# Random-feature attention, a dense four-expert layer and a cosine layer on one core: float64 weight halves spaced by TensorE columns instead of by quanta

## The chip, the cores and the metric

The kernel runs on one core of one Trainium2 chip. The metric is the device time of one execution in microseconds (us). Five engines work side by side, each through its own list of instructions in order: TensorE (PE in the profile, PEld its weight loads), VectorE (DVE), ScalarE (ACT), GpSimd (POOL) and SyncE (SP). GpSimd's and SyncE's queues also issue DMA transfers between the chip's memory and the on-chip buffer. An instruction that has to wait holds up all that stand behind it in its engine's list.

## The reference, cut to what matters

```
q_p, k_p = phi(q), phi(k)                     # phi(x) = exp(h - max h) / sqrt(m), h = x omega^T - |x|^2 / 2
attn = (q_p (k_p^T v)) / (q_p sum(k_p) + 1e-6)       # 2 x 8 heads x 576 tokens x 64
x = attn.reshape(1152, 512)
p = domain_probs / (sum(domain_probs) + 1e-9)
out = 0
for e in range(4):
    out += p[:, e] * (relu(x @ w1[e]) @ w2[e])       # 512 -> 1024 -> 512
h = out @ w_in                                       # 512 -> 2048, w_in is float64
result = (h * cos(h)) @ w_out                        # 2048 -> 512, w_out is float64
```

All inputs are float32, but `w_in` and `w_out` are float64. Each factor of a product is split into a high and a low part, and three products (high by high, high by low, low by high) stand for one.

## The kernel before

After the attention part, TensorE goes through six **rounds** of the same shape: rounds 0 to 3 are the four experts, rounds 4 and 5 the two halves of the cosine layer's 2048 hidden columns (`E = 4`). From round 1 on a round has two parts. **Part one** (`first_product`) makes the hidden values, 1152 tokens in three chunks of 384; seven products and two plain ones per pair of hidden blocks take the place of a plain block product, so VectorE adds their results into `h` (L449), some from banks that TensorE opens again later (`g_..c`). **Part two** (`Second`) multiplies by the second weight: for each of nine token tiles of 128, ScalarE makes the high part `sth` (L523) of a half of the hidden values and VectorE the low part `stl` (L524), up to two or three halves ahead; TensorE's third matmul of a half reads `stl`. VectorE adds the result into `acc` (L584).

The program is written by generators. Each `yield` on TensorE's stream is a **quantum** of six matmuls: 6 x 384 = 2304 columns in part one, 6 x 512 = 3072 columns in part two. Part one has 44 quanta, part two 36, a round 80 (round 0 has 84). `plan()` names for each background job the quantum at which it starts; from then on it advances one `yield` per quantum. So the order of each engine's list is fixed by these numbers, and the engines run through it as their waits allow. Below, "quantum 41" of a round counts from its first; 0 to 43 are part one.

The background jobs are these. `load_v2` and `load_a` bring the next experts' weights through SP and split them (ScalarE L106, VectorE L108); `load_a` also makes the sums of weight blocks that the seven products need (four additions on L140, a split on L106 and L108). `convert64` turns the float64 weights into float32: 32 **halves** of 128 x 512 numbers, 512 KB each. Halves of kind `a` are of `w_in`, those of kind `v` of `w_out`. A half goes like this:

- quantum q: GpSimd's queue issues the load of `f64r` (L176 or L182)
- q + 5 (`LEAD`): ScalarE copies the absolute value of the high words out of `f64r` into `f64t` (L186). In this text that is *the copy* of a half
- one quantum later VectorE's L190 and L193, two later L198 and L201, three later L204, the last reader of `f64r`; for kind `a` also L209, and one quantum later the store `ka` (L211)
- kind `v` only: five quanta behind the copy ScalarE makes the high part from `f64a` into `f64t` (L215); six behind, VectorE makes the low part in `f64b` (L217, L218), and the two stores `kv_..h` and `kv_..l` are issued (L220)

There is one buffer each of `f64r`, `f64t`, `f64a` and `f64b` (pool `c1`, `bufs=1`; two halves of round 0 use a second pool). A load therefore waits for L204 of the half before it, and a copy waits for the store that still reads `f64t`. The eight halves of round 0 have written-out quanta. The other 24 start at quantum 80 of round 0, spaced 8 quanta apart for kind `a` (`A_GAP`) and 10 for kind `v` (`V_GAP`); eight `v` halves fall into round 1, eight `a` halves into round 2, eight `v` halves into the end of round 2 and round 3.

Of the kernel before, what the change touches and what calls it, by code (L numbers as in the profile page):

```python
# [26 lines left out]
def performer_moe_kernel(ctx, tc, q, k, v, omega, probs, w1, w2, w_in, w_out, out):  # L27
    nc = tc.nc
# [14 lines left out]
    CW = TC * P  # L43
# [16 lines left out]
    late = {}  # L60
# [31 lines left out]
        return units[key]  # L92

    LEAD = 5
    A_GAP, V_GAP = 8, 10

    def wait(n):
        for _ in range(n):
            yield
# [55 lines left out]

    kept = {}

    def convert64(pool, key, z):

        kind, e, u = key
        n = UW // 2
        hf = e - E
        if key not in kept:
            nm = "_".join(map(str, key))
            kept[key] = (
                dram.tile([P, UW], F32, tag=f"k{nm}", name=f"k{nm}")
                if kind == "a"
                else tuple(dram.tile([P, UW], F32, tag=f"k{nm}{s}", name=f"k{nm}{s}") for s in "hl")  # L170
            )
        raw = pool.tile([P, n, 2], U32, tag="f64r", name="f64r")
        lw, hw = raw[:, :, 0], raw[:, :, 1]
        if kind == "a":
            c0 = hf * F + (z * NPF + u) * P
            nc.gpsimd.dma_start(  # L176
                out=raw.rearrange("p (k f) t -> p k f t", f=P),
                in_=w_in32[:, c0 : c0 + P, :].rearrange("(k p) f t -> p k f t", p=P),
            )
        else:  # L180
            r0 = hf * F + u * 256 + z * P
            nc.gpsimd.dma_start(out=raw, in_=w_out32[r0 : r0 + P, :, :])  # L182
        yield from wait(LEAD)

        t = pool.tile([P, n], U32, tag="f64t", name="f64t")
        nc.scalar.activation(t.bitcast(F32), hw.bitcast(F32), ACTF.Abs)  # L186
        yield
        a = pool.tile([P, n], U32, tag="f64a", name="f64a")
        b = pool.tile([P, n], F32, tag="f64b", name="f64b")
        nc.vector.tensor_scalar(  # L190
            out=t.bitcast(F32), in0=t.bitcast(F32), scalar1=2.0**-15, scalar2=None, op0=ALU.max
        )
        nc.vector.tensor_scalar(  # L193
            out=a, in0=t, scalar1=0x07FFFFFF, scalar2=3,
            op0=ALU.bitwise_and, op1=ALU.logical_shift_left,
        )
        yield
        nc.vector.scalar_tensor_tensor(  # L198
            out=a, in0=hw, scalar=0xC0000000, in1=a, op0=ALU.bitwise_and, op1=ALU.bitwise_or
        )  # L200
        nc.vector.tensor_scalar(out=t, in0=a, scalar1=0xFF800000, scalar2=None, op0=ALU.bitwise_and)  # L201
        yield
        af = a.bitcast(F32)
        nc.vector.scalar_tensor_tensor(  # L204
            out=b, in0=lw, scalar=2.0**-52, in1=t.bitcast(F32), op0=ALU.mult, op1=ALU.mult
        )
        half = slice(z * n, (z + 1) * n)
        if kind == "a":
            nc.vector.tensor_tensor(out=af, in0=af, in1=b, op=ALU.add)  # L209
            yield  # L210
            nc.gpsimd.dma_start(out=kept[key][:, half], in_=af)  # L211
            return
        yield from wait(2)
        hi = t.bitcast(F32)
        nc.scalar.activation(t.bitcast(F32R), af, ACTF.Copy)  # L215
        yield
        nc.vector.tensor_tensor(out=af, in0=af, in1=hi, op=ALU.subtract)  # L217
        nc.vector.tensor_tensor(out=b.bitcast(F32R), in0=af, in1=b, op=ALU.add)  # L218
        for part, dst in zip((hi, b), kept[key]):
            nc.gpsimd.dma_start(out=dst[:, half], in_=part)  # L220

    def load_v64(e, u):

# [412 lines left out]
    QE = [84] + (E + 1) * [80]  # L636
    starts = [{} for _ in range(E + 2)]

    def start_at(e, q, make, *args):
        while q >= QE[e]:  # L640
            q -= QE[e]
            e += 1
        starts[e].setdefault(q, []).append(lambda: make(*args))

    def plan():
        start_at(0, 45, token_sums)
        start_at(0, 60, token_sum3)
        for e in range(1, E + 2):
            for p, q in enumerate((60, 70) if e == 1 else (50, 60)):
                start_at(e - 1, q, load_a, e, p)  # L650
            start_at(e, 0, load_v2 if e < E else load_v64, e, 0)
            start_at(e, 6, load_a, e, 2)
            start_at(e, 9, load_v2 if e < E else load_v64, e, 1)
            start_at(e, 17, load_a, e, 3)
            start_at(e, 23, load_v2 if e < E else load_v64, e, 2)
            start_at(e, 26, load_v2 if e < E else load_v64, e, 3)

        halves = [
            (kind, e, u, z)
            for e in (E, E + 1) for kind in "av" for u in range(NU) for z in range(2)  # L660
        ]
        when = [(q, "c1") for q in (21, 31, 41, 51, 61, 71)] + [(q, "c2") for q in (23, 33)]
        n = len(halves) - len(when)
        gaps = [A_GAP if h[0] == "a" else V_GAP for h in halves[len(when) :]]
        when += [(80 + sum(gaps[:i]), "c1") for i in range(n)]
        for (kind, e, u, z), (q, ring_) in zip(halves, sorted(when)):
            start_at(0, q, lambda k=(kind, e, u), z=z, r=ring_: convert64(late[r], k, z))
        start_at(E - 1, 58, second_x, 1)
        start_at(E - 1, 69, second_sums)
        start_at(E, 3, second_x, 0)  # L670

    plan()

    def dense():
# [39 lines left out]
    with tc.tile_pool(name="at1", bufs=1) as at1, tc.tile_pool(name="at2", bufs=2) as at2:  # L714
# [280 lines left out]
        for b in range(B):  # L995
            nc.sync.dma_start(
                out=pr[:, b * R : (b + 1) * R, :],
                in_=probs[b * S : b * S + SB, :].rearrange("(p r) e -> p r e", r=R),
            )
            nc.sync.dma_start(  # L1000
                out=pr[b * L : (b + 1) * L, NTILE - 1, :], in_=probs[b * S + SB : (b + 1) * S, :]
# [48 lines left out]
        for s in range(NPR + 3):  # L1050
# [39 lines left out]
            if 2 <= s <= NPR + 1:  # L1090
                b, hp = pairs[s - 2]
# [29 lines left out]
            if s == 1:  # L1121
# [4 lines left out]
                    out=pn, in0=pr, in1=psum_.to_broadcast([P, NTILE, E]), op=ALU.mult  # L1126
# [38 lines left out]
```

## Time and profile before

| what | value |
|---|---|
| median of 3 runs | 679.45 us (678.39 to 679.77) |
| the profiled execution's own time | 678.58 us |
| its span, first to last instruction | 676.8 us |
| TensorE busy | 664.8 us (98%) |
| VectorE busy | 513.5 us (76%) |
| ScalarE busy | 314.1 us (46%) |
| GpSimd busy | 169.5 us (25%) |
| granted TensorE clock, mean | 0.999 |

The page gives busy times; matmuls overlap in the pipeline, so that 98% busy does not mean that no time is lost: a short stop between two matmuls is covered by the recorded length of the first. The view of windows cuts the span at given times; the windows below are cut at the first matmul of a part, so that the length of a window is what the part took. The view of waits names, for an engine that stood idle, the instruction or the transfer that released it. The timeline shows single instructions with their start, their length and, in brackets, the idle time ahead of them.

### The profile page before, as it was taken

To read this page: it belongs to the slowest core of one execution; us is meant where nothing else is said; L and a number is where in the kernel's file an instruction comes from. 1 tells how busy PE (TensorE), PEld (TensorE's weight loads), DVE (VectorE), ACT (ScalarE), POOL (GpSimd) and SP (SyncE) were. 2 spreads that over 40 slices of the span, in tenths; PEclk is the share of its full clock that TensorE was granted. 3 is DMA by queue.
4 is the path that set the end of the run, shared out by engine and by line. 5 is a ranking of instruction groups with operands and counts; after the bars stand their busy time and mean duration, and the time that the engine had idled before them with its cause. 6 is when DMAs were issued, how large, how long until landed. Compare 5 with 4: busy or idle time off the path is not lost.

```text
span 676.8 us, 10000 instructions
## 1 busy us (share of the span) xinstructions
PE 664.8 (98%) x3665; PEld 608.3 (90%) x3665; DVE 513.5 (76%) x945; ACT 314.1 (46%) x626; POOL 169.5 (25%) x220
## 2 busy tenths in 40 slices
PE   8999999999999899999899999999999999999998
PEld 7999998998899888899787899888999888999887
DVE  6998645788867779679677789788778785396962
ACT  4777763244243344335324245454355664355540
POOL 8778420110111111111110111100034340143420
PEclk9999999999999999999999999999999999999999
DMA  8654001233444624427433536320711000700111
GB/s 196 182 140 124 33 1 63 94 105 114 118 131 125 214 67 138 142 57 209 124 94 79 166 119 196 110 78 17 279 59 36 1 0 4 308 1 1 47 47 47
DMA packets 51217, 68.86 MB, mean 102 GB/s; under 512 B 15072, under 2 KB 35808, under 8 KB 51168
## 3 DMA queue, kind: packets, MB, share of 16 engines
q1 hardware_dynamic: 42576, 38.82, 18.4%
q0 software_dynamic: 8448, 29.37, 14.1%
q8 instruction: 29, 0.48, 0.3%
q14 instruction: 20, 0.16, 0.1%
q10 hardware_dynamic: 144, 0.03, 0.0%
HBM read 53.27 MB, written 14.94 MB: 101 GB/s over the span
## 4 chain that ended last, share of the span: by engine, by line
PE 78%; DVE 10%; DMA 6%; issue 3%; ACT 2%; POOL 0%; POOLq 0%; ACTq 0%; DVEq 0%
PE g L551 37%; PE g L402 15%; DMA f64r<-in_moe_w_in_dram 3%; PE num L936 2%; PE kv L907 2%; DVE h L449 2%; PE pj_q L830 1%; PE g_0a L402 1%; PE g_0c L402 1%; DVE f64a L198 1%; PE g_1c L402 1%; PE g_1a L402 1%; PE pj_k L830 1%; DVE f64b L204 1%; PE g_3c L402 1%
## 5 line engine op out<-in xcount | busy, mean ns | idle before, releaser
L523 ACT ACTIVATE sth<-h 128x512 fp32r<-128x512 f32 x72 | 44.6, 629 | 51.9 <-PE g L551 48.8
L524 DVE SCALAR_TENSOR_TENSOR stl<-h,sth 128x512 fp32r<-128x512 f32 x72 | 48.8, 685 | 17.3 <-ACT sth L523 17.1
L186 ACT ACTIVATE f64t<-f64r 128x512 f32<-128x512 f32 x32 | 21.3, 666 | 66.3 <-DMA f64r<-in_moe_w_in_dram 33.6
L551 PE MATMUL g<-v_0h,stl 128*128 128x512 f32 (+1 forms) x110 | 43.2, 393 | 4.7 <-DVE stl L524 4.7
L108 DVE TENSOR_TENSOR stl<-h,sth 128x512 fp32r<-128x512 f32 x36 | 35.3, 983 | 13.8 <-ACT sth L106 13.8
L551 PE MATMUL g<-v_3h,sth 128*128 128x512 f32 (+1 forms) x110 | 42.7, 388 | 0.0
L551 PE MATMUL g<-v_0h,sth 128*128 128x512 f32 (+1 forms) x110 | 42.6, 387 | 0.0
L551 PE MATMUL g<-v_2h,stl 128*128 128x512 f32 (+1 forms) x110 | 42.6, 387 | 0.0
L551 PE MATMUL g<-v_2h,sth 128*128 128x512 f32 (+1 forms) x110 | 42.5, 386 | 0.0
L551 PE MATMUL g<-v_0l,sth 128*128 128x512 f32 (+1 forms) x110 | 42.5, 386 | 0.0
L551 PE MATMUL g<-v_1h,stl 128*128 128x512 f32 (+1 forms) x110 | 42.4, 386 | 0.0
L551 PE MATMUL g<-v_1h,sth 128*128 128x512 f32 (+1 forms) x110 | 42.4, 386 | 0.0
L551 PE MATMUL g<-v_3h,stl 128*128 128x512 f32 (+1 forms) x110 | 42.4, 386 | 0.0
L551 PE MATMUL g<-v_1l,sth 128*128 128x512 f32 (+1 forms) x110 | 42.4, 386 | 0.0
L551 PE MATMUL g<-v_2l,sth 128*128 128x512 f32 (+1 forms) x110 | 42.4, 385 | 0.0
L551 PE MATMUL g<-v_3l,sth 128*128 128x512 f32 (+1 forms) x110 | 42.4, 385 | 0.0
L343 ACT ACTIVATE h<-g 128x384 f32<-128x384 f32 x48 | 23.2, 487 | 39.2 <-PE g L402 39.0
L182 POOL DMA_DIRECT2D f64r<-in_moe_w_out_dram x16 | 8.6, 539 | 120.5 <-DVE f64b L204 67.1
L353 POOL TENSOR_TENSOR cosa<-cosa,cosr 128x384 f32<-128x384 f32 x16 | 18.7, 1171 | 78.3 <-DVE cosr L350 78.3
L176 POOL DMA_DIRECT2D f64r<-in_moe_w_in_dram x16 | 12.3, 770 | 78.6 <-DVE f64b L204 59.7
L551 PEld LDWEIGHTS g<-v_0h,stl 128*128 128x128 f32 x110 | 20.6, 188 | 11.3 <-DVE stl L524 7.3
L106 ACT ACTIVATE sth<-h 128x512 fp32r<-128x512 f32 x36 | 22.4, 623 | 16.1 <-PE g L551 12.5
(407 smaller groups left out, 2134.3 us busy)
## 6 DMA issues: line engine op xcount, KB each, us to landing
ra<-in_moe_w_dram SPq DMA_DIRECT2D x32, 256.0 KB, 3.3
rv<-in_moe_w_dram SPq DMA_DIRECT2D x16, 512.0 KB, 3.8
f64r<-in_moe_w_in_dram POOLq DMA_DIRECT2D x16, 512.0 KB, 4.5
f64r<-in_moe_w_out_dram POOLq DMA_DIRECT2D x16, 512.0 KB, 4.4
ka<-f64a POOLq DMA_DIRECT2D x16, 256.0 KB, 4.1
ra<-ka SPq DMA_DIRECT2D x8, 512.0 KB, 4.2
kt<-in_k_dram SPq DMA_DIRECT2D x8, 256.0 KB, 2.9
qt<-in_q_dram SPq DMA_DIRECT2D x8, 256.0 KB, 3.3
```

What stands on the lines that cost most here:

```text
L106: nc.scalar.activation(hi, src, ACTF.Copy)
L108: eng.tensor_tensor(out=lo, in0=src, in1=hi.bitcast(F32), op=ALU.subtract)
L186: nc.scalar.activation(t.bitcast(F32), hw.bitcast(F32), ACTF.Abs)
L343: nc.scalar.activation(dst, src, ACTF.Copy)
L353: nc.gpsimd.tensor_tensor(out=vv, in0=vv, in1=kk, op=ALU.subtract)
L402: nc.tensor.matmul(dst, x[:, o], y[:, kk, :], start=start and n == 0, stop=stop and n == 3 * kn - 1, skip_group_check=reopen,)
L449: nc.vector.tensor_tensor(out=dst, in0=x, in1=y, op=ALU.add)
L523: nc.scalar.activation(hi, src, ACTF.Relu)
L524: nc.vector.scalar_tensor_tensor(out=lo, in0=src, scalar=0.0, in1=hi.bitcast(F32), op0=ALU.max, op1=ALU.subtract)
L551: nc.tensor.matmul(g, x[:, p, :], y[:, o : o + w], start=n == 0, stop=n == 3 * FT - 1)
L830: nc.tensor.matmul(pj[:, i * 256 : (i + 1) * 256], a[:, cs], b_, start=z == 0, stop=z == 2)
L907: nc.tensor.matmul(kvp[:, h, :], phk[:, h * R + r, :], ve[:, h * R + r, :], start=r == 0, stop=r == R - 1)
```

## The change

A half is no longer spaced by quanta but by columns of TensorE's work. `columns_to(q)` counts the columns that TensorE has before quantum q, `quantum_at(columns)` finds the first quantum at or behind a number of columns, both counted from quantum 80 of round 0. The starts of the 24 later halves are 22000 columns apart for kind `a` and 26000 for kind `v`, and their copy stands 14000 columns behind their load, instead of five quanta. The halves of round 0 ahead of quantum 80 stay as they are. In rounds 1 to 3 the loads thus move by -1 to +5 quanta, and the time from load to copy is 5 to 7 quanta. The store of the high part is issued in the program right behind L215 and not behind L218; in the new file the lines below the removed one have numbers lower by one (L217 and L218 keep theirs).

```diff
--- before.py
+++ after.py
@@ -92,7 +92,6 @@
         return units[key]
 
     LEAD = 5
-    A_GAP, V_GAP = 8, 10
 
     def wait(n):
         for _ in range(n):
@@ -155,7 +154,7 @@
 
     kept = {}
 
-    def convert64(pool, key, z):
+    def convert64(pool, key, z, lead):
 
 
 
@@ -180,7 +179,7 @@
         else:
             r0 = hf * F + u * 256 + z * P
             nc.gpsimd.dma_start(out=raw, in_=w_out32[r0 : r0 + P, :, :])
-        yield from wait(LEAD)
+        yield from wait(lead)
 
         t = pool.tile([P, n], U32, tag="f64t", name="f64t")
         nc.scalar.activation(t.bitcast(F32), hw.bitcast(F32), ACTF.Abs)
@@ -213,11 +212,11 @@
         yield from wait(2)
         hi = t.bitcast(F32)
         nc.scalar.activation(t.bitcast(F32R), af, ACTF.Copy)
+        nc.gpsimd.dma_start(out=kept[key][0][:, half], in_=hi)
         yield
         nc.vector.tensor_tensor(out=af, in0=af, in1=hi, op=ALU.subtract)
         nc.vector.tensor_tensor(out=b.bitcast(F32R), in0=af, in1=b, op=ALU.add)
-        for part, dst in zip((hi, b), kept[key]):
-            nc.gpsimd.dma_start(out=dst[:, half], in_=part)
+        nc.gpsimd.dma_start(out=kept[key][1][:, half], in_=b)
 
     def load_v64(e, u):
 
@@ -636,6 +635,15 @@
     QE = [84] + (E + 1) * [80]
     starts = [{} for _ in range(E + 2)]
 
+    A_GAP, V_GAP, LOAD64 = 22000, 26000, 14000
+
+    def columns_to(q):
+        full, q = divmod(q - 84, 80)
+        return (full * 80 + q + max(0, q - 44) / 3 + full * 12) * 6 * CW
+
+    def quantum_at(columns):
+        return next(q for q in range(80, sum(QE)) if columns_to(q) - columns_to(80) >= columns)
+
     def start_at(e, q, make, *args):
         while q >= QE[e]:
             q -= QE[e]
@@ -662,9 +670,10 @@
         when = [(q, "c1") for q in (21, 31, 41, 51, 61, 71)] + [(q, "c2") for q in (23, 33)]
         n = len(halves) - len(when)
         gaps = [A_GAP if h[0] == "a" else V_GAP for h in halves[len(when) :]]
-        when += [(80 + sum(gaps[:i]), "c1") for i in range(n)]
+        when += [(quantum_at(sum(gaps[:i])), "c1") for i in range(n)]
         for (kind, e, u, z), (q, ring_) in zip(halves, sorted(when)):
-            start_at(0, q, lambda k=(kind, e, u), z=z, r=ring_: convert64(late[r], k, z))
+            lead = LEAD if q < 80 else quantum_at(columns_to(q) - columns_to(80) + LOAD64) - q
+            start_at(0, q, lambda k=(kind, e, u), z=z, r=ring_, l=lead: convert64(late[r], k, z, l))
         start_at(E - 1, 58, second_x, 1)
         start_at(E - 1, 69, second_sums)
         start_at(E, 3, second_x, 0)
```

How the lists move, at three places. First ScalarE's list at the end of part one and the start of part two of round 2: `h10`, `h00` and `h01` are hidden values, `sth` the high parts for part two, and the rows that write `f64t` are the copies of two halves of `w_in`. Before:

```order
L453 ACTIVATE h10_3278<-g1_2_3a_3638 128x384
L186 ACTIVATE f64t_3646<-f64r_3602 128x512
L343 ACTIVATE h00_3276<-g1_2_0_0_3_3691 128x384
L523 ACTIVATE sth_3705<-h00_3276 128x512
L343 ACTIVATE h01_3277<-g1_2_0_1_3_3709 128x384
L523 ACTIVATE sth_3723<-h01_3277 128x512
L186 ACTIVATE f64t_3727<-f64r_3680 128x512
L365 ACTIVATE h10_3278<-g1_2_3a_3638 128x384
L523 ACTIVATE sth_3756<-h00_3276 128x512
L523 ACTIVATE sth_3778<-h01_3277 128x512
L523 ACTIVATE sth_3796<-h00_3276 128x512
```

Now:

```order
L452 ACTIVATE h10_3278<-g1_2_3a_3637 128x384
L342 ACTIVATE h00_3276<-g1_2_0_0_3_3678 128x384
L522 ACTIVATE sth_3692<-h00_3276 128x512
L185 ACTIVATE f64t_3696<-f64r_3635 128x512
L342 ACTIVATE h01_3277<-g1_2_0_1_3_3698 128x384
L522 ACTIVATE sth_3716<-h01_3277 128x512
L364 ACTIVATE h10_3278<-g1_2_3a_3637 128x384
L522 ACTIVATE sth_3748<-h00_3276 128x512
L522 ACTIVATE sth_3764<-h01_3277 128x512
L185 ACTIVATE f64t_3775<-f64r_3722 128x512
L522 ACTIVATE sth_3784<-h00_3276 128x512
```

The first of the two copies stood ahead of the first `sth` and stands behind it; the second one has moved from between the second and third `sth` to ahead of the fifth.

Second, VectorE's list in part two of round 2, from the sum into `acc2` on: `rs3_0` are the sums of weight blocks for round 3, `stl` the low parts that TensorE waits for, and `f64t`, `f64a` and `f64b` belong to a half. Before:

```order
L584 SCALAR_TENSOR_TENSOR acc2_85<-g2_2_2_0_3834,pn_86,acc2_85 128x512
L140 TENSOR_TENSOR rs3_0_3876<-ra3_0_3822 128x256
L140 TENSOR_TENSOR rs3_0_3876<-rs3_0_3876,ra3_0_3822 128x256
L524 SCALAR_TENSOR_TENSOR stl_3887<-h10_3278,sth_3886 128x512
L140 TENSOR_TENSOR rs3_0_3876<-ra3_0_3822 128x256
L140 TENSOR_TENSOR rs3_0_3876<-ra3_0_3822,rs3_0_3876 128x256
L108 TENSOR_TENSOR a_3_0l_3874<-ra3_0_3822,a_3_0h_3873 128x1024
L524 SCALAR_TENSOR_TENSOR stl_3908<-h11_3279,sth_3907 128x512
L190 TENSOR_SCALAR f64t_3899<-f64t_3899 128x512
L193 TENSOR_SCALAR f64a_3914<-f64t_3899 128x512
L584 SCALAR_TENSOR_TENSOR acc3_1730<-g2_2_3_0_3879,pn_86,acc3_1730 128x512
L108 TENSOR_TENSOR s_3_0l_3912<-rs3_0_3876,s_3_0h_3911 128x1024
```

Now:

```order
L583 SCALAR_TENSOR_TENSOR acc2_85<-g2_2_2_0_3826,pn_86,acc2_85 128x512
L189 TENSOR_SCALAR f64t_3853<-f64t_3853 128x512
L192 TENSOR_SCALAR f64a_3862<-f64t_3853 128x512
L139 TENSOR_TENSOR rs3_0_3869<-ra3_0_3815 128x256
L139 TENSOR_TENSOR rs3_0_3869<-rs3_0_3869,ra3_0_3815 128x256
L523 SCALAR_TENSOR_TENSOR stl_3880<-h10_3278,sth_3879 128x512
L197 SCALAR_TENSOR_TENSOR f64a_3862<-f64r_3801,f64a_3862 128x512
L200 TENSOR_SCALAR f64t_3853<-f64a_3862 128x512
L139 TENSOR_TENSOR rs3_0_3869<-ra3_0_3815 128x256
L139 TENSOR_TENSOR rs3_0_3869<-ra3_0_3815,rs3_0_3869 128x256
L203 SCALAR_TENSOR_TENSOR f64b_3863<-f64r_3801,f64t_3853 128x512
L208 TENSOR_TENSOR f64a_3862<-f64a_3862,f64b_3863 128x512
```

The five instructions of a half up to the one that writes `f64b` stand between the four additions into `rs3_0`; before, they came behind them.

Third, GpSimd's queue at the start of round 1: `f64r` are loads of halves, `kv_..h` and `kv_..l` the stores of the high and the low part. Before:

```order
L182 DMA f64r_2492<-in_moe2_w_out_dram 128x1024
L220 DMA kv_4_0h_2390<-f64t_2437 128x512
L220 DMA kv_4_0l_2391<-f64b_2448 128x512
L182 DMA f64r_2604<-in_moe2_w_out_dram 128x1024
L220 DMA kv_4_0h_2390<-f64t_2542 128x512
L220 DMA kv_4_0l_2391<-f64b_2555 128x512
L182 DMA f64r_2715<-in_moe2_w_out_dram 128x1024
L220 DMA kv_4_1h_2602<-f64t_2648 128x512
```

Now:

```order
L215 DMA kv_4_0h_2390<-f64t_2437 128x512
L181 DMA f64r_2493<-in_moe2_w_out_dram 128x1024
L219 DMA kv_4_0l_2391<-f64b_2448 128x512
L215 DMA kv_4_0h_2390<-f64t_2561 128x512
L181 DMA f64r_2622<-in_moe2_w_out_dram 128x1024
L219 DMA kv_4_0l_2391<-f64b_2575 128x512
L181 DMA f64r_2739<-in_moe2_w_out_dram 128x1024
L215 DMA kv_4_1h_2620<-f64t_2694 128x512
```

The first two stores of a high part stand ahead of a load that they stood behind; the third still stands behind it.

## Rows read from the trace of the kernel before

**Rows 1.** Windows: stretch, length; busy time (count) of PE, PEld, DVE, ACT, POOL; clock, DMA.

```profile
186.56:233.92 47.36, 46.39 (x266) 45.75 (x265) 36.62 (x63) 20.40 (x33) 6.16 (x12) 1.00 0.48 144
233.92:284.42 50.50, 49.56 (x217) 40.39 (x217) 40.14 (x69) 19.47 (x30) 7.21 (x13) 1.00 0.43 135
284.42:330.24 45.82, 45.82 (x265) 45.81 (x264) 37.52 (x66) 19.14 (x30) 5.28 (x9) 1.00 0.45 127
330.24:384.17 53.93, 50.16 (x218) 40.24 (x217) 39.75 (x70) 17.00 (x27) 6.45 (x11) 1.00 0.38 108
384.17:429.95 45.78, 45.78 (x265) 45.78 (x264) 39.70 (x67) 21.52 (x34) 7.55 (x14) 1.00 0.48 151
528.98:578.10 49.12, 49.12 (x217) 40.47 (x217) 33.58 (x51) 26.50 (x50) 12.64 (x10) 1.00 0.06 22
```

**Rows 2.** TensorE's waits, whole span: microseconds in total, times, longest.

```profile
PE g L551 <- DVE stl L524: 4.7, 6, 1.4
...
PE g_2c L402 <- DVE h L449: 0.6, 1, 0.6
```

**Rows 3.** ScalarE's waits from 284 to 384 us (round 2).

```profile
ACT f64t L186 <- DMA f64r<-in_moe_w_in_dram: 26.3, 7, 6.8
```

**Rows 4.** ScalarE's waits from 186.56 to 284 us (round 1).

```profile
ACT f64t L186 <- DMA kv_0h<-f64t: 4.3, 2, 4.2
```

**Rows 5.** Timeline of ScalarE, copies of halves: start, length, what, [idle before, releaser].

```profile
325.38 0.67 ACT L186 ACTIVATE f64t<-f64r 128x512 f32<-128x512 f32 x1 [4.88 <-DMA f64r<-in_moe_w_in_dram]
...
334.70 0.66 ACT L186 ACTIVATE f64t<-f64r 128x512 f32<-128x512 f32 x1 [5.21 <-DMA f64r<-in_moe_w_in_dram]
...
344.10 0.66 ACT L186 ACTIVATE f64t<-f64r 128x512 f32<-128x512 f32 x1 [6.80 <-DMA f64r<-in_moe_w_in_dram]
...
354.84 0.66 ACT L186 ACTIVATE f64t<-f64r 128x512 f32<-128x512 f32 x1 [5.21 <-DMA f64r<-in_moe_w_in_dram]
...
366.73 0.66 ACT L186 ACTIVATE f64t<-f64r 128x512 f32<-128x512 f32 x1 [5.29 <-DMA f64r<-in_moe_w_out_dram]
...
423.91 0.66 ACT L186 ACTIVATE f64t<-f64r 128x512 f32<-128x512 f32 x1 [3.57 <-DVE h L449]
```

**Rows 6.** Timeline of GpSimd: loads of halves and a store.

```profile
206.75 0.54 POOL L182 DMA_DIRECT2D f64r<-in_moe_w_out_dram  x1 [8.25 <-DVE h L449]
...
207.28 0.54 POOL L220 DMA_DIRECT2D kv_0h<-f64t  x1
...
362.17 0.54 POOL L182 DMA_DIRECT2D f64r<-in_moe_w_out_dram  x1 [10.57 <-DVE f64b L204]
```

**Rows 7.** Timeline of VectorE, second part of round 2.

```profile
353.36 0.42 DVE L140 TENSOR_TENSOR rs<-ra,rs 128x256 f32<-128x256 f32 x1
...
356.66 0.42 DVE L190 TENSOR_SCALAR f64t<-f64t 128x512 f32<-128x512 f32 x1
...
357.46 0.75 DVE L584 SCALAR_TENSOR_TENSOR acc<-g,pn,acc 128x512 f32<-128x512 f32 x1
...
358.12 1.22 DVE L108 TENSOR_TENSOR s_0l<-rs,s_0h 128x1024 fp32r<-128x1024 f32 x1
...
359.25 0.69 DVE L198 SCALAR_TENSOR_TENSOR f64a<-f64r,f64a 128x512 uint32<-128x512 uint32 x1
...
360.32 0.68 DVE L524 SCALAR_TENSOR_TENSOR stl<-h,sth 128x512 fp32r<-128x512 f32 x1
...
360.92 0.68 DVE L204 SCALAR_TENSOR_TENSOR f64b<-f64r,f64t 128x512 f32<-128x512 uint32 x1
```

**Rows 8.** Timeline of TensorE around its longest stop in part two of round 2.

```profile
336.76 0.39 PE L551 MATMUL g<-v_0l,sth 128*128 128x512 f32 x1
...
338.46 0.50 PE L551 MATMUL g<-v_0h,stl 128*128 128x512 f32 x1 [1.31 <-DVE stl L524]
```

**Rows 9.** DMA issues: engine, operation, count, KB each, median us to landing.

```profile
f64r<-in_moe_w_in_dram POOLq DMA_DIRECT2D x16, 512.0 KB, 4.5
...
kv_0h<-f64t POOLq DMA_DIRECT2D x4, 256.0 KB, 5.2
```

## The prediction

> **What bounds the kernel now.** I read the windows first, then who made TensorE wait, then whom that engine waited for.
>
> Cut at the first matmul of a part, the windows show that TensorE runs its parts at a fixed pace except in three of them. Part one takes 45.82 us in round 2 and 45.78 in round 3, so its floor is 45.80, or 1.041 us a quantum; part two takes 49.12 us in round 4, where no half is converted, or 1.364 us a quantum [rows 1]. Over these floors stand part one of round 1 by 47.36 - 45.80 = 1.56 us, part two of round 1 by 50.50 - 49.12 = 1.38, and part two of round 2 by 53.93 - 49.12 = 4.81. Together 7.75 us. This is all that a better order of background work can give back in these rounds; the granted clock is 1.00 in every one of them.
>
> The reader is to see next that it is `stl`, VectorE's low part, that TensorE waits for (4.7 us that the view shows, six times), and in part one a sum on L449 [rows 2]. The view shows less than the windows, since a recorded matmul (0.39 us, [rows 8]) is longer than TensorE's pace of 49.12 / 216 = 0.23 us a matmul and covers the start of a stop. VectorE in turn is late because ScalarE is: in round 2 ScalarE stood idle for 26.3 us, seven times, at the copy of a half, for the load of `f64r` [rows 3]. All `sth` of part two stand in the same list behind that copy.
>
> Why are the loads late? Follow one half around. Its copy starts at 354.84 [rows 5]; VectorE's L204 ends at 360.92 + 0.68 = 361.60 [rows 7]; GpSimd, which waited for just that, issues the next load at 362.17 [rows 6]; the next copy starts at 366.73 [rows 5]. From the end of L204 to the next copy it is 5.13 us, of which the transfer takes 4.5 [rows 9]. The whole cycle took 9.32 us (325.38 to 334.70), then 9.40, 10.74 and 11.89 [rows 5]. The program gives it 8 quanta: 8.33 us in part one, 10.91 in part two. So in part one each half falls one microsecond further behind. The copy at 334.70 stands at quantum 41 of round 2, which TensorE reaches at 284.42 + 41 x 1.041 = 327.1 [rows 1]: it is 7.6 us late. Right behind it TensorE has its longest stop, 1.31 us idle at 338.46 [rows 8]. In part two the cycle fills the time it has, so the lateness stays.
>
> How late may a copy be? In round 3 the copy at quantum 35 stands at 423.91, against 384.17 + 35 x 1.041 = 420.6: 3.3 us late, and that part is at its floor [rows 1, 5]. So 3.3 us cost nothing, 7.6 us cost about 2.
>
> **The change part by part.**
>
> *Halves of `w_in` in part one of round 2.* 22000 columns are 9.5 quanta, so the copies come to stand at quanta 0, 10, 20, 29 and 39: 9.4 to 10.4 us apart, against a cycle of 9.3 to 9.4. From L204 (three quanta behind a copy) to the next copy there are 6 or 7 quanta, 6.2 to 7.3 us for the 5.13 that are needed; before there were 5 quanta, 5.2 us. The lateness that grew by a microsecond a half no longer grows. I take at most 1 us at the end of part one, from VectorE's other work. With it goes the stop at the start of part two: no stop there.
>
> *Halves of `w_out` in round 1.* Here the copy waits for the store of the high part too (4.3 us in two waits) [rows 4]. That store is issued right behind a load, at 207.28 after 206.75 [rows 6], and lands 5.2 us later [rows 9]; the next copy stood five quanta (5.2 us) behind L215 in part one. With 26000 columns (11.3 quanta) it stands six or seven behind, 6.2 to 7.3 us. So the 1.56 us of part one go, and the lateness that part two inherits.
>
> *The high half stored at once.* In the trace that store follows the load directly already, while the low part is still being made; the earlier line only swaps the two issues where L215 and a load fall into one quantum. That costs the load one issue of 0.54 us [rows 6] and gives the store as much. Taken at nothing; its bounds are 0.54 us either way on a copy, which 3.3 us of room cover.
>
> *The other side: part two gets more.* The same 22000 columns are only 7.2 quanta of part two, 26000 only 8.5. In part two of round 2 the copies stand at 47, 54, 61 and 68: from L204 to the next copy 4 quanta, 5.46 us, against 6.82 before. The spare time over 5.13 falls from 1.7 to 0.3 us. In the new order (the second place shown in the change) the half whose copy is at 54 has four of the additions on L140 and one `stl` between its own instructions. Sum up to L204: five of its own, 3 x 0.42 + 0.69 + 0.68; four additions, 4 x 0.42; one `stl`, 0.68; together 4.99 [rows 7]. With the copy (0.66) and the 5.13 back to the next copy that is 10.8 us, for 7 x 1.364 = 9.55: 1.2 us late. The half at 61 has one sum into `acc` (0.75) and one `stl` in between: 4.06 + 0.66 + 5.13 = 9.85, another 0.3. With the 1 us inherited the copy at 68 is 2.5 us late, within the 3.3 that cost nothing.
>
> What can still stop TensorE there is VectorE itself. In quanta 55 to 59 stand the splits and sums for round 3 (4 x 0.42 + 2 x 1.22 = 4.12), a whole half (3.3) and five quanta of `stl` and `acc` ((2 x 0.68 + 0.75) x 5/4 = 2.6) [rows 7]: 10.0 us of work in 6.8, so VectorE falls 3.2 us back. An `stl` is asked for three quanta (4.1 us) ahead of its half and read 0.45 us into it (two matmuls); less 0.6 for `sth` and 0.7 for itself that leaves 3.2 us of cover. It is just used up, and a late ScalarE comes on top. I leave 0.8 us of stops in round 2 and 0.2 us in round 1, where copies at 55 and 63 meet the same work with one load less. Bounds: none at all, or the 4.8 us that part two of round 2 loses now.
>
> For the landing of a half's load there is a rule in the Trainium skill, "DMA: Bandwidth & Descriptors", section "Anatomy of one DMA — SWDGE (gpsimd) path": about 2.0 us plus the bytes over 436 GB/s. An estimate by that page gives 3.2 us for 512 KB; the row says 4.5 [rows 9], and the cycle at 354.84 bears the row out. By the rule the half at 54 would need 9.5 us and just fit, so that the stops left would be nearer to none; I go by the row.
>
> *Sum.* 7.75 - 1.0 = 6.75 us less. The profiled execution took 678.58 us (span 676.8, and 1.8 around it, which stay); it comes to 671.8. It lay 0.9 below the median of 679.45, so the median comes to **672.7**. Work is neither added nor removed; rounds 0, 4 and 5 do not move.
>
> **The rivals.**
>
> *All stops go.* The spare time in part two is enough. For it: in round 3 the engines carry 3.3 us without loss. Against: VectorE has 10 us of work in 6.8. Time: 679.45 - 7.75 = 671.7.
>
> *Part two keeps its stops.* A cycle of 10.74 and 11.89 us as now, in a place of 9.55, makes the copies at 54, 61 and 68 later by 1.2 to 2.3 us each, some 5 us in all, which is past 3.3. Then part two of round 2 keeps half of its 4.81 and that of round 1 half of its 1.38: 679.45 - 7.75 + 3.1 = 674.8. For it: these are measured cycles. Against: they were measured with ScalarE 7 us behind, so that VectorE got its work in lumps.
>
> *The waits at the copy are harmless and VectorE's lumps are the cause.* Then the spacing changes nothing but where they fall: 679.4. Against: in round 3, with the same splits and sums, no stop in part one.
>
> *Slower: VectorE's backlog at the splits of part two.* Before, a half's instructions lay mostly beside these bursts (quanta 55 to 59 and 65 to 69 of rounds 1 and 2); now they lie in all four. If staging covers nothing, each stops TensorE for the 3.2 us of backlog: 12.8 - 7.75 = 5.0 us slower, 684.5. It is slower from 1.9 us per burst on. Against: the longest stop in the trace, with ScalarE 7.6 us late, was 1.31 idle [rows 8].
>
> **How the numbers follow.** The forecast has a chance of 0.46 (its own range 672.0 to 674.0), all stops gone 0.18, part two keeping its stops 0.20, no change 0.08, slower 0.08. What a measurement can tell from no change is 0.2%, or 1.4 us. The first three are faster: 0.84. The range starts below the second by the spread of the runs (0.7 us) and reaches past the third to 677.0.
>
> **What would show it.** In the new profile part one of round 1 at 45.8 us and part two of round 2 near 50; ScalarE's wait for `f64r` in round 2 down from 26.3 us to under 10; the copies of round 2 within 3 us of their quanta; the store of the high part no longer a wait of more than 2 us. It is wrong if the cycle of a half takes longer than 10 us in part one, or if TensorE waits for `stl` at quanta 55 to 70.

## The result, and the profile after

The changed kernel takes 671.44 us (median of 4 runs, 671.10 to 671.71) against 678.92 for the kernel before (4 runs, 678.26 to 679.77): the ratio is 0.9889 (95% interval 0.9872 to 0.9906), 7.5 us less. The forecast was 672.7 us, 6.75 us less than the kernel before. The time lies in the range 671.0 to 677.0.

The page of the new kernel, its span and its busy times:

```profile
span 669.6 us, 9996 instructions
...
PE 662.9 (99%) x3665; PEld 608.0 (91%) x3665; DVE 513.0 (77%) x945; ACT 314.7 (47%) x626; POOL 169.5 (25%) x220
```
The work is the same; the span is 7.2 us shorter. The windows, cut at the first matmul of a part like those of [rows 1] (columns as there; the last row is part two of round 4), show where:

```profile
186.58:232.36 45.78, 45.78 (x265) 45.78 (x264) 37.53 (x65) 21.42 (x34) 5.62 (x11) 1.00 0.46 149
232.36:281.66 49.30, 49.30 (x217) 40.48 (x217) 39.60 (x68) 18.85 (x29) 7.73 (x14) 1.00 0.39 120
281.66:327.45 45.79, 45.79 (x265) 45.78 (x264) 37.05 (x65) 20.12 (x32) 5.19 (x9) 1.00 0.47 147
327.45:376.95 49.50, 49.29 (x217) 40.47 (x217) 38.83 (x67) 16.06 (x26) 6.56 (x11) 1.00 0.39 118
376.95:422.74 45.79, 45.79 (x266) 45.79 (x265) 38.70 (x66) 20.66 (x34) 6.46 (x12) 1.00 0.51 150
521.76:570.89 49.13, 49.13 (x217) 40.47 (x217) 33.58 (x51) 26.50 (x50) 12.64 (x10) 1.00 0.06 22
```
Part one of round 1 went from 47.36 to 45.78, part two from 50.50 to 49.30, part two of round 2 from 53.93 to 49.50: 1.58 + 1.20 + 4.43 = 7.21 us, all of the difference in span. Nothing else moved. ScalarE's wait at the copies in round 2, 26.3 us in seven times before [rows 3], is now this (total, times, longest):

```profile
ACT f64t L185 <- DMA f64r<-in_moe_w_in_dram: 13.7, 6, 4.0
```
Of the stops, the largest that is left is in part two of round 2. Three timelines answer to [rows 5], [rows 7] and [rows 8]: ScalarE's copies, VectorE up to the late `stl`, TensorE.

```profile
344.96 0.66 ACT L185 ACTIVATE f64t<-f64r 128x512 f32<-128x512 f32 x1 [3.26 <-DMA f64r<-in_moe_w_in_dram]
...
355.33 0.67 ACT L185 ACTIVATE f64t<-f64r 128x512 f32<-128x512 f32 x1 [4.04 <-DMA f64r<-in_moe_w_in_dram]
...
366.05 0.68 ACT L185 ACTIVATE f64t<-f64r 128x512 f32<-128x512 f32 x1 [1.22 <-DMA f64r<-in_moe_w_out_dram]
```
```profile
349.26 0.42 DVE L139 TENSOR_TENSOR rs<-ra,rs 128x256 f32<-128x256 f32 x1
349.59 0.68 DVE L203 SCALAR_TENSOR_TENSOR f64b<-f64r,f64t 128x512 f32<-128x512 uint32 x1
...
350.92 1.22 DVE L107 TENSOR_TENSOR a_0l<-ra,a_0h 128x1024 fp32r<-128x1024 f32 x1
352.05 0.68 DVE L523 SCALAR_TENSOR_TENSOR stl<-h,sth 128x512 fp32r<-128x512 f32 x1
```
```profile
352.20 0.39 PE L550 MATMUL g<-v_2l,sth 128*128 128x512 f32 x1
352.79 0.50 PE L550 MATMUL g<-v_2h,stl 128*128 128x512 f32 x1 [0.21 <-DVE stl L523]
```
The copies stand at quanta 54, 61 and 68, which TensorE reaches at 327.45 + 10, 17 and 24 x 1.364 us = 341.1, 350.6 and 360.2. They are 3.9, 4.7 and 5.9 us late: each falls about one microsecond further behind. The lateness does not begin there: the first copy of round 2 starts at 284.59, 2.9 us behind its quantum, and the one at quantum 39 at 324.55, 2.3 us behind. The last of the four additions on L139 stands ahead of the half's L203, and the split on L107 ahead of `stl`. TensorE stands for 0.36 us there (0.59 between two starts, 0.23 being its pace), at quantum 62.

### The profile page after: what moved, and what is told of

Its sections match the earlier page's. It is cut to its first block, busy times and chain, and to the rows that moved or that the text cites. A ratio compares the mean times of both kernels' runs of the same rounds, so it can differ in the third digit from the quotient of the medians.

```text
span 669.6 us, 9996 instructions
## 1 busy us (share of the span) xinstructions
PE 662.9 (99%) x3665; PEld 608.0 (91%) x3665; DVE 513.0 (77%) x945; ACT 314.7 (47%) x626; POOL 169.5 (25%) x220
## 4 chain that ended last, share of the span: by engine, by line
PE 93%; DVE 3%; DMA 1%; POOL 1%; ACT 1%; issue 0%; POOLq 0%; DVEq 0%; ACTq 0%
PE g L550 42%; PE g L401 20%; PE num L945 2%; PE kv L916 2%; PE g_0a L401 2%; PE g_0c L401 2%; PE g_3c L401 2%; PE g_3a L401 2%; PE g_2c L401 2%; PE g_2a L401 2%; PE g_1c L401 2%; PE g_1a L401 2%; PE pj_q L839 1%; PE pj_k L839 1%; PE tq L929 1%; PE g_0e L401 1%
## 5 line engine op out<-in xcount | busy, mean ns | idle before, releaser
L107 DVE TENSOR_TENSOR stl<-h,sth 128x512 fp32r<-128x512 f32 x36 | 35.3, 983 | 13.8 <-ACT sth L105 13.8
L175 POOL DMA_DIRECT2D f64r<-in_moe_w_in_dram x16 | 12.3, 770 | 78.4 <-DVE f64b L203 48.8
L583 DVE SCALAR_TENSOR_TENSOR acc<-g,pn,acc 128x512 f32<-128x512 f32 x27 | 20.2, 746 | 13.2 <-PE g L550 13.2
```

The costliest lines, as they stand in the source:

```text
L107: eng.tensor_tensor(out=lo, in0=src, in1=hi.bitcast(F32), op=ALU.subtract)
L583: nc.vector.scalar_tensor_tensor(out=acc[t], in0=src, scalar=p_, in1=acc[t], op0=ALU.mult, op1=ALU.add)
```

## The experiments

My theory was that a half's cycle (copy, VectorE up to L204, load, landing, next copy) must fit into the spacing of the copies. Rival one: what helps is the longer time from load to copy. Rival two: what counts is where VectorE's instructions fall. Rival three: the store at once. All times are medians beside runs of the kernel before on the same chip.

**Gaps alone.** The copy again stands five quanta behind its load.

```diff
-            lead = LEAD if q < 80 else quantum_at(columns_to(q) - columns_to(80) + LOAD64) - q
+            lead = LEAD
```

> The changed kernel, but every copy stands five quanta behind its load as before; the spacing of the loads stays at 22000 and 26000 columns. My theory (a half's cycle from copy to L204 to load to copy must fit into the spacing of the copies): the copies are still 22000 columns apart, so the time is that of the changed kernel, 671.5 to 672.5 us. Rival one (the earlier load is what helps): most of the gain goes, 676 to 679 us. Rival two (it is where VectorE's lumps fall): the copies move by one or two quanta, 672 to 675 us.

Measured: 678.41 us, ratio 0.9981 (0.9967 to 0.9995). Nearly all the gain is gone, and my theory as I had put it missed. In its profile part one of rounds 1 and 2 is still at its floor; the time is lost in part two of both and in round 3 (the rows: part two of rounds 1 and 2, the two parts of round 3, of which the changed kernel takes 45.79 and 51.77 us):

```profile
232.50:283.75 51.25, 50.60 (x218) 40.09 (x217) 40.60 (x69) 19.89 (x32) 8.27 (x15) 1.00 0.36 115
...
329.53:380.12 50.59, 49.94 (x217) 40.11 (x217) 39.72 (x68) 17.27 (x28) 6.63 (x11) 1.00 0.39 115
380.12:428.10 47.98, 45.95 (x266) 45.63 (x264) 37.77 (x65) 20.65 (x33) 6.49 (x12) 1.00 0.45 143
428.10:481.83 53.73, 53.73 (x240) 44.13 (x241) 46.91 (x77) 23.04 (x37) 4.34 (x8) 0.97 0.20 69
```

**Lead alone.** The loads are 8 and 10 quanta apart again, the copies stay 14000 columns behind.

```diff
-    A_GAP, V_GAP, LOAD64 = 22000, 26000, 14000
+    A_GAP, V_GAP, LOAD64 = 8, 10, 14000
-        when += [(quantum_at(sum(gaps[:i])), "c1") for i in range(n)]
+        when += [(80 + sum(gaps[:i]), "c1") for i in range(n)]
```

> The changed kernel, but the loads are 8 and 10 quanta apart as before; the copy stays 14000 columns behind its load. My theory: the copies of w_in are again 8.33 us apart in part one for a cycle of 9.3, whatever their distance from the load in the program, since the load waits for L204: 678 to 680 us, with ScalarE's wait for f64r in round 2 at 20 us or more. Rival one (the earlier load): 671.5 to 673 us.

Measured: 682.91 us, ratio 1.0049 (1.0034 to 1.0064): slower than before, with 24.5 us of ScalarE's waits for `f64r` of `w_in` in round 2. So neither part does it alone, and rival one falls. Both kernels keep the store at once.

**Store alone.** The kernel before, with only the store of the high part issued right behind L215.

```diff
         nc.scalar.activation(t.bitcast(F32R), af, ACTF.Copy)
+        nc.gpsimd.dma_start(out=kept[key][0][:, half], in_=hi)
         yield
-        for part, dst in zip((hi, b), kept[key]):
-            nc.gpsimd.dma_start(out=dst[:, half], in_=part)
+        nc.gpsimd.dma_start(out=kept[key][1][:, half], in_=b)
```

> The kernel before, with only the store of the high part issued right behind L215. My theory: nothing, 678.5 to 679.5 us, since in the trace the store already follows the load directly. Rival three (the store is what holds the copy in round 1): round 1 gives back its 2.8 us, 676 us.

Measured: 680.44 us, ratio 1.0018 (1.0004 to 1.0031): slower. That was the hint. GpSimd's queue in round 1, and the L204 that the load needs, in this kernel:

```profile
207.75 0.54 POOL L216 DMA_DIRECT2D kv_0h<-f64t  x1 [9.11 <-ACT f64t L215]
208.30 0.54 POOL L182 DMA_DIRECT2D f64r<-in_moe_w_out_dram  x1
```
```profile
206.11 0.68 DVE L204 SCALAR_TENSOR_TENSOR f64b<-f64r,f64t 128x512 f32<-128x512 uint32 x1
```
L204 ends at 206.79, but the load goes out at 208.30, 1.5 us later: the store stands ahead of it in GpSimd's list and waits for L215. Before, the load went out first, 0.57 us after L204, and the store behind it [rows 6]. The same view for the kernel with the gaps alone:

```profile
207.46 0.54 POOL L215 DMA_DIRECT2D kv_0h<-f64t  x1 [8.96 <-ACT f64t L214]
210.86 0.54 POOL L219 DMA_DIRECT2D kv_0l<-f64b  x1 [2.85 <-DVE f64b L218]
211.39 0.54 POOL L181 DMA_DIRECT2D f64r<-in_moe_w_out_dram  x1
```
```profile
205.82 0.68 DVE L203 SCALAR_TENSOR_TENSOR f64b<-f64r,f64t 128x512 f32<-128x512 uint32 x1
...
209.87 0.69 DVE L218 TENSOR_TENSOR f64b<-f64a,f64b 128x512 fp32r<-128x512 f32 x1
```
Here the load stands behind both stores, and the second waits for L218, which ends at 210.56. From the end of L204 (206.50) to the load it is 4.9 us. So the cycle has a term that I had left out: how long the load waits in GpSimd's list behind the stores. The distance from load to copy sets the load's place in that list. With 22000 - 14000 = 8000 columns (3.5 quanta) from a copy to the next load, the load of kind `a` stands ahead of the store `ka` (four quanta behind the copy); with five quanta instead it stands behind it, and in the gaps alone four loads of round 2 go out behind `ka`, 1.6 us after L204.

**Gaps, load first.** To test that: the kernel with the gaps alone, copies still five quanta behind the load, and only the stores written later: `ka` and the low part by two quanta, the high part by three.

```diff
             nc.vector.tensor_tensor(out=af, in0=af, in1=b, op=ALU.add)
-            yield
+            yield from wait(3)
             nc.gpsimd.dma_start(out=kept[key][:, half], in_=af)
...
-        nc.gpsimd.dma_start(out=kept[key][0][:, half], in_=hi)
...
-        nc.gpsimd.dma_start(out=kept[key][1][:, half], in_=b)
+        yield from wait(2)
+        for part, dst in zip((hi, b), kept[key]):
+            nc.gpsimd.dma_start(out=dst[:, half], in_=part)
```

> The run with the gaps alone (copies five quanta behind the load, 678.4 us), with one thing changed: the stores of a half are written two quanta later, so that the next load stands ahead of them in GpSimd's list. Theory: the distance from load to copy matters only because it sets where the load stands in GpSimd's list; with the load ahead of the stores it follows L204 in 0.57 us and the time is 671.3 to 672.8 us. Rival (a copy five quanta behind its load comes before the transfer has landed, whatever the list): 677 to 679 us, as with the gaps alone.

Measured: 671.08 us, ratio 0.9879 (0.9864 to 0.9894): the whole gain, and 7.3 us less than with the gaps alone. GpSimd's queue at the same place, and the windows of part two of rounds 1 and 2:

```profile
206.61 0.54 POOL L181 DMA_DIRECT2D f64r<-in_moe_w_out_dram  x1 [8.69 <-DVE h L449]
207.14 0.54 POOL L220 DMA_DIRECT2D kv_0h<-f64t  x1
```
```profile
232.26:281.54 49.28, 49.28 (x218) 40.48 (x217) 38.99 (x67) 18.65 (x29) 7.20 (x13) 1.00 0.38 119
...
327.32:376.33 49.01, 49.01 (x218) 40.56 (x218) 38.91 (x67) 17.20 (x27) 6.56 (x11) 1.00 0.40 119
```
The load goes out first, 0.57 us after L204 (206.04), and part two of round 2 takes 49.01 us: no stop at all. So the 14000 columns are not needed as time for the transfer; they work through the order of the list.

**Store late.** The changed kernel with both stores behind L218 again.

```diff
-        nc.gpsimd.dma_start(out=kept[key][0][:, half], in_=hi)
...
-        nc.gpsimd.dma_start(out=kept[key][1][:, half], in_=b)
+        for part, dst in zip((hi, b), kept[key]):
+            nc.gpsimd.dma_start(out=dst[:, half], in_=part)
```

> The changed kernel, with the store of the high part issued behind L218 again, as before. The runs so far say that GpSimd's list holds the load of the next half back where a store stands ahead of it: in the kernel with the store at once alone the load came 1.0 to 1.5 us after the end of L204, against 0.57 before. By that theory every load now follows its L204 in 0.57 us, the copies of round 1 are less late, and there is little left to gain: 670.8 to 671.6 us. If the store at once was worth something, 672 us or more.

Measured: 671.39 us, ratio 0.9884 (0.9867 to 0.9900). As the changed kernel: within it the store at once neither helps nor hurts.

**Only the halves of `w_in`, only those of `w_out`.** The others keep 10 or 8 quanta and five quanta to the copy.

```diff
+    COLS = "a"        # the second kernel: "v"
+            if h[0] in COLS:
+                q = quantum_at(columns_to(q) - columns_to(80) + (A_GAP if h[0] == "a" else V_GAP))
+            else:
+                q += 8 if h[0] == "a" else 10
-            lead = LEAD if q < 80 else ...
+            lead = LEAD if q < 80 or kind not in COLS else ...
```

> Only the halves of w_in (round 2) are spaced by columns and have their copy 14000 columns behind; those of w_out stay at 10 quanta with the copy five quanta behind. The store at once is in. My theory: round 2 gives back its 4.4 us and round 1 keeps its stops of 2.8: 674 to 675.5 us. If the two rounds hang together (round 2 inherits its lateness from round 1), round 2 keeps a stop of 1 us or more: 675.5 to 677 us.

> Only the halves of w_out (rounds 1 and 3) are spaced by columns, with their copy 14000 columns behind the load; those of w_in stay at 8 quanta with the copy five quanta behind. Theory: round 1 gives back its 2.8 us, round 2 keeps its 4.4 to 4.8: 675.5 to 677 us. If round 2 only stops because of what it inherits from round 1, 672 to 674 us.

Measured: 675.49 us, ratio 0.9946 (0.9929 to 0.9962), and 677.35 us, ratio 0.9974 (0.9963 to 0.9985). Each brings its own round; in the first, part two of round 2 is free of stops while part two of round 1 is longer than before (52.02 against 50.50). The store at once is in this kernel, and its halves of `w_out` keep the old spacing, as in the run with the store alone. In both profiles round 1 is longer than before, 98.46 us here and 98.91 there against 97.86, but in the run with the store alone it is part one that is longer (49.87 us), and part two takes 49.04. So the longer part two cannot be put down to the store; the same lists stopped TensorE at different places in two executions. One difference is a transfer: ScalarE's copy waited for the load of the same half, issued at 208.30 there and 208.48 here, until 215.22 there and 213.21 here:

```profile
233.13:285.15 52.02, 49.84 (x217) 40.31 (x217) 40.01 (x68) 19.30 (x30) 7.27 (x13) 1.00 0.42 128
...
330.94:379.94 49.00, 49.00 (x217) 40.54 (x217) 38.88 (x66) 17.55 (x26) 4.99 (x8) 1.00 0.34 100
```
**Longer load.** The changed kernel; each load of a half of `w_in` in round 2 is followed by a second load of its first quarter.

```diff
+            if e > E:
+                nc.gpsimd.dma_start(out=raw[:, :P, :], in_=w_in32[:P, c0 : c0 + P, :])
```

> The changed kernel, where each load of a half of w_in for round 5 (the eight halves converted in round 2) is followed by a second load of its first quarter into the same place, which waits for the first: the values stay the same. VectorE's and ScalarE's lists are those of the changed kernel. Theory (the cycle of a half must fit into its spacing): the cycle grows by 2.5 to 3.5 us, from 9.4 to about 12.3 in a spacing of 9.5 to 10.4, so each copy falls 2 to 3 us further behind, 15 us by the middle of part two, and round 2 is 6 us or more longer: 676 to 686 us. Rival (VectorE's lumps alone make TensorE stop): 671 to 672.5 us.

Measured: 694.29 us, ratio 1.0221 (1.0206 to 1.0236), further than expected: the copies of `w_in` are 11.6 to 15.2 us apart, where I had expected a cycle of 12.3. The two parts of round 2, and ScalarE's wait in it:

```profile
281.54:337.44 55.90, 48.53 (x265) 47.25 (x264) 35.53 (x61) 16.95 (x27) 7.88 (x13) 0.97 0.40 121
337.44:400.21 62.77, 52.58 (x217) 39.55 (x217) 40.17 (x70) 18.00 (x30) 9.26 (x16) 1.00 0.36 109
```
```profile
ACT f64t L187 <- DMA f64r<-in_moe_w_in_dram: 50.1, 7, 8.7
```
VectorE and ScalarE have the lists of the changed kernel, and the round is 118.67 us long instead of 95.29. So a longer cycle makes stops with VectorE's instructions where they were. The edit lengthens more than the transfer: the second load waits 3.6 to 3.9 us in GpSimd's list for the first, and `ka` stands behind it.

**Tighter.** 19200 columns instead of 22000 for `w_in`.

```diff
-    A_GAP, V_GAP, LOAD64 = 22000, 26000, 14000
+    A_GAP, V_GAP, LOAD64 = 19200, 26000, 14000
```

> The changed kernel with the halves of w_in 19200 columns apart instead of 22000: 8.7 us in part one and 8.5 in part two of round 2, against a cycle of 9.3 to 10.8 us. Theory: each copy falls 0.6 us further behind in part one and 0.6 to 2 in part two, to 7 or 8 us late in part two, and TensorE stops there for 2 to 5 us: 673.5 to 676.5 us. If the distance from load to copy was what helped: 671.3 to 672.3 us.

Measured: 679.62 us, ratio 1.0005 (0.9996 to 1.0015): all of the gain is gone. Round 2:

```profile
281.66:327.45 45.79, 45.79 (x266) 45.78 (x265) 37.80 (x66) 19.46 (x31) 5.20 (x9) 1.00 0.50 147
327.45:384.92 57.47, 52.79 (x217) 39.37 (x217) 41.45 (x72) 17.08 (x27) 8.19 (x14) 1.00 0.41 116
```
Part one is still at its floor, part two is 8.35 us over that of 49.12. By TensorE's pace without stops its copies at quanta 48 and 55 are 8.7 and 8.8 us late. The direction is that of the theory; my 2 to 5 us were too few. VectorE's instructions move with the copies here, so this run alone does not rule out rival two.

**Nine quanta, without and with the load first.** The kernel before with one number changed, then also with the stores two quanta later.

```diff
-    A_GAP, V_GAP = 8, 10
+    A_GAP, V_GAP = 9, 10
# the second kernel also:
-            yield
+            yield from wait(3)
             nc.gpsimd.dma_start(out=kept[key][:, half], in_=af)
+        yield from wait(2)
         for part, dst in zip((hi, b), kept[key]):
```

> The kernel before with one number changed: the halves of w_in 9 quanta apart instead of 8, still by quanta and with the copy five quanta behind. Nine quanta are 9.4 us in part one and 12.3 in part two, for a cycle of 9.3 to 9.4 and 10.7 to 11.9. Theory: round 2 gives back most of its 4.4 to 4.8 us and round 1 keeps its 2.8: 674.5 to 676 us. If it takes columns, so that both parts are filled alike, 677 us or more.

> The run with nine quanta (679.9 us), with the stores of a half written two quanta later, so that the next load stands ahead of the store ka in GpSimd's list. In that run the load came 1.6 us after the end of L204, behind ka, and the cycle was 10 us and more in a spacing of 9.4. Theory: the load follows L204 in 0.57 us again, the cycle of 9.3 fits into part one, round 2 gives back 3 to 4.5 us, while the halves of w_out keep the stops of round 1 and may bring some in round 3, where they stand at other quanta: 674.5 to 677.5 us. If quanta as a spacing are at fault and not the list, 679 us or more.

Measured: 679.90 us, ratio 1.0014 (1.0000 to 1.0028), a miss, and 677.29 us, ratio 0.9973 (0.9961 to 0.9985). GpSimd's queue in the first and the L204 before it (its end: 303.79), then the queue in the second:

```profile
304.81 0.54 POOL L211 DMA_DIRECT2D ka<-f64a  x1 [10.16 <-DVE f64a L209]
305.38 0.76 POOL L176 DMA_DIRECT2D f64r<-in_moe_w_in_dram  x1
```
```profile
303.11 0.68 DVE L204 SCALAR_TENSOR_TENSOR f64b<-f64r,f64t 128x512 f32<-128x512 uint32 x1
```
```profile
303.30 0.76 POOL L176 DMA_DIRECT2D f64r<-in_moe_w_in_dram  x1 [9.64 <-ACT s_2h L106]
304.05 0.54 POOL L211 DMA_DIRECT2D ka<-f64a  x1
```
At nine quanta the load falls behind `ka` (1.6 us after L204), and a spacing of 9.4 us no longer holds the cycle. That is only a part of the miss: in this profile round 2 takes 97.76 us, 2.0 less than before, while part one of round 3 takes 4.0 more (the rows: both parts of round 2, part one of round 3):

```profile
285.02:332.49 47.47, 46.25 (x265) 45.60 (x263) 35.92 (x63) 17.68 (x29) 5.21 (x8) 1.00 0.41 122
332.49:382.78 50.29, 50.07 (x216) 40.34 (x217) 38.84 (x66) 18.01 (x28) 6.05 (x10) 1.00 0.30 95
382.78:432.58 49.80, 47.63 (x266) 47.31 (x264) 40.19 (x69) 20.41 (x33) 6.72 (x13) 0.97 0.48 149
```
With the load first, round 2 is at its floors with plain quanta, though VectorE's list in it is the same; so rival two does not explain these stops:

```profile
284.50:330.29 45.79, 45.79 (x266) 45.78 (x264) 36.94 (x64) 18.82 (x31) 5.19 (x8) 1.00 0.44 127
330.29:379.29 49.00, 49.00 (x218) 40.55 (x217) 38.01 (x65) 17.29 (x26) 6.04 (x10) 1.00 0.34 99
379.29:426.74 47.45, 46.08 (x265) 45.76 (x264) 39.34 (x68) 19.92 (x32) 6.48 (x12) 1.00 0.47 145
```
The rows are the same three parts. What still costs time are the halves of `w_out`: part one of round 1 takes 47.23 us as before, and round 3, where they now stand at other quanta, goes from 45.78 to 47.45. Their copies at quanta 23 and 33 of round 3 are 4.7 and 6.2 us late, against 3.3 at quantum 35 before. So for `w_out` at 10 quanta it matters at which quantum a half falls, and rival two may keep a part. Whether the work does it that VectorE has there, or the store that these two copies wait for (3.1 and 2.9 us), was not tried.

## Why the prediction was right

**The floors and the sum.** Right: the 7.75 us over the floors were what there was, and 7.2 came back, each part near its forecast.

**The cycle as the cause.** Right in its core: spacing, transfer time and list order each decide by whether the cycle fits (tighter, longer load, nine quanta). But the cycle was incomplete. The step "from L204 to the next copy 5.13 us" holds only while the load is the first thing that GpSimd's list can do; in the runs it grew by 0.9 to 4.3 us where a store stood ahead. Nor is the cycle as even as the 9.32 and 9.40 us from which I took it: the copies in the first half of part one of round 2 stood 10.78 and 10.08 us apart before (286.07, 296.85 and 306.93), the later two waiting for their transfers.

**Halves of `w_out` in round 1.** The 1.56 us of part one came back, but the cause that I named, the copy's wait for the store, does not make a stop by itself. In the run with the gaps and the load first ScalarE's copies wait 13.9 us for stores in round 1, against 11.2 before, and both parts are free of stops. What goes with the stops is how late a copy is: up to 8.3 us in round 1 before (227.15, at quantum 31), at most 4.3 in that run and 3.5 in the changed kernel.

**The high half stored at once, "taken at nothing".** This step was wrong. I took the price of two swapped issues, 0.54 us; but on a list in order the load inherits the store's wait for L215. Alone it costs 1.2 us (0.3 to 2.1). In the changed kernel it touches few loads; one of them:

```profile
209.83 0.54 POOL L215 DMA_DIRECT2D kv_0h<-f64t  x1 [11.52 <-ACT f64t L214]
210.38 0.54 POOL L181 DMA_DIRECT2D f64r<-in_moe_w_out_dram  x1
```
**The copy 14000 columns behind.** I counted it as time that the transfer has. It is that only in name: with the wider spacing it keeps the load ahead of the stores, where the old spacing had it anyway (three quanta from a copy to the next load for `w_in`, five for `w_out`). Without it the gain is 0.9 us instead of 7.5.

**Part two of round 2.** The direction was right, two terms of the lateness were too small. I put the copies at most 1 us late at the end of part one; they were 2.3, since they came into round 2 already 2.9 late. From quantum 54 on I had 1.2 and 0.3 us a half and measured 0.8 and 1.1, and the half at 47, for which I had nothing, added 0.9. So at quantum 68 it was 5.9 us and not 2.5. That this cost 0.4 us and not more says that the room is wider than the 3.3 us that I had read from one row. The two errors met, which is luck: part two of round 2 is 0.4 us over the floor of 49.12 that I used, instead of 0.8. So three of the signs that I named failed, though the time did not: ScalarE's wait for `f64r` is 13.7 us and not under 10, copies are later than 3 us, and ScalarE still waits three times for a store of the high part for more than 2 us (2.9, 4.2 and 4.5). Both signs of being wrong came as well: a cycle of 10.59 us in part one of round 2 (copies at 294.09 and 304.68, the second waiting for its transfer), which the spacing of 10.4 us nearly held, and the stop for `stl` at quantum 62. The first was badly chosen, as the kernel before had such cycles already. Part one at 45.8 and part two near 50 held.

**The rivals.** All stops gone was nearly the case (671.7; the run with the load first has it): with 671.44 us the result lies nearer to this rival than to the forecast. Slower by VectorE's backlog did not happen, nor did part two keep its stops.

**The rule on a load's landing.** By the Trainium skill, "DMA: Bandwidth & Descriptors", section "Anatomy of one DMA — SWDGE (gpsimd) path", a half would land in 3.2 us, an estimate from its fit. The copy at 355.33 of the changed kernel waited for a transfer; its load in GpSimd's queue:

```profile
350.85 0.76 POOL L175 DMA_DIRECT2D f64r<-in_moe_w_in_dram  x1 [9.36 <-ACT s_0h L105]
```
That is 4.48 us, as in [rows 9]; the trace does not agree with the rule. By the rule part two would have had room for 1.3 us more a half, and the copies there would not have fallen behind.

## What to carry to other kernels

Where a buffer is used in a ring, write down the whole cycle, and put the queue that issues the transfer into it: a load that stands behind a store in an in-order list waits for what the store waits for. Then ask in each stage of the program whether the cycle fits the spacing; an even spacing in steps of the program is uneven in time where the steps differ in length. A number that seems to buy time may work by the order that it makes, so test it with the order held.

## What the runs showed of the hardware that I had not expected

A long stop costs more than itself. In the run with only `w_out` by columns, TensorE stood idle for 2.71 us at the start of part two of round 2. The window behind it (the third number from the end is the granted clock), then TensorE's timeline:

```profile
332.00:336.00 4.00, 3.73 (x9) 2.94 (x10) 1.28 (x3) 0.05 (x1) 0.75 (x2) 0.57 0.66 197
```
```profile
329.15 0.40 PE L550 MATMUL g<-v_0l,sth 128*128 128x512 f32 x1
332.27 0.70 PE L550 MATMUL g<-v_0h,stl 128*128 128x512 f32 x1 [2.71 <-DVE stl L523]
332.77 0.63 PE L550 MATMUL g<-v_0h,sth 128*128 128x512 f32 x1
333.20 0.63 PE L550 MATMUL g<-v_0l,sth 128*128 128x512 f32 x1
```
After the stop the matmuls start 0.43 us apart instead of 0.23, and the clock granted from 332 to 336 us is 0.57: for a part of that stretch the lower of the two levels, 1.2 instead of 2.4 GHz. Eight matmuls at 0.2 us more are 1.6 us on top of the stop. Behind the 1.31 us idle of [rows 8] no such stretch follows: the granted clock is 1.00 from 338.46 to 342.46 us. The kernel with the gaps alone, whose profile has such a stretch too (0.69 from 428.10 to 432.00 us, behind 2.03 us idle), scatters from 675.95 to 680.14; the changed kernel from 671.10 to 671.71. Its runs show that much of this is the clock, which falls in some executions and not in others: six have a mean granted clock of 0.996 or 0.997 and take 678.05 to 680.14 us, four have 1.00 and take 675.95 to 678.21. The medians are 678.9 and 676.7, and a mean clock lower by 0.003 is 2.0 us over a span of 677. So in the executions where it falls, some 2 us of what the gaps alone lose are not the stops themselves but the clock behind them (an estimate from these figures). With the store alone, the six runs at 0.999 or 1.00 have a median of 679.4, hardly more than the 679.3 before, and the four at 0.997 one of 681.6.
